# Seven block products for eight in a feed-forward layer: attention and two feed-forward blocks on one core

## Chip, core and metric

The kernel runs on one NeuronCore of a Trainium2 chip. TensorE (PE) multiplies matrices into PSUM, VectorE (DVE) and ScalarE (ACT) do the element-wise work, GpSimd (POOL) helps in the attention part, SyncE (SP) issues most DMAs. The metric is the device time of one execution in microseconds; lower is better.

## What is computed

Attention over 2 batches and 8 heads (query rows averaged in pairs, 576 queries against 1152 keys, head size 64) gives x of 1152 tokens by 512. Two feed-forward blocks follow:

```python
# first block
h = x @ w_in                      # 512 -> 2048
P = a[0] + a[1]*h + a[2]*h**2 + a[3]*h**3
Q = 1 + |b[0]|*|h| + |b[1]|*h**2
x = (P / (Q + 1e-6)) @ w_out      # 2048 -> 512
# second block
h = x @ w_in2                     # 512 -> 2048
g = max(h, 0) + log1p(exp(-|h|))  # softplus
out = g @ w_out2                  # 2048 -> 512
```

The four weight matrices arrive as 64-bit floats; each is turned on the chip into fp32.

## The kernel before

All products of the feed-forward blocks are made of two-part numbers. A value v is kept as `hi`, its rounding to the matmul type fp32r, and `lo`, the rest v - hi. A product a·b is three matmuls: hi·hi, lo·hi, hi·lo. Tokens are cut into three chunks c of 384 (`TOK`), the 2048 hidden columns into 16 slices f of 128 (`NF`), the 512 model columns into four slices d of 128 (`ND`).

The second block is the stage that the change touches. Its loop (line 1494) goes over 48 units (c, f). For one unit `up2` (L1343) makes h of 128 x 384 in one PSUM bank by 12 matmuls of 384 columns (four d times three). `act2` then has ScalarE take the softplus out of PSUM (L1351) and cast it to `gh` (L1352), and VectorE subtract to `gl` (L607, called through `sub`). Two units later `down2` (L1365) multiplies: for each of three token tiles t, three matmuls of 512 columns into the accumulator `acc[c, t]`. Units come as chunks 2 and 1 for f 0 to 7, chunk 0 for f 0 to 7, then f 8 to 15 chunk by chunk. `half2` puts the sums of chunks 1 and 2 after eight f into SBUF (L1374, L1376), and `end2` adds them in at the end (L1386) and sends the result out (L1391). Of the eight PSUM banks two hold h tiles (pool `ph2`) and six hold accumulators (`pa2`).

Weights come one tile (one f of w_in2 or w_out2) at a time while the loop runs. `w_load` (L643, L648) brings 512 KB into one of two staging tiles `wraw`; `w_abs` has ScalarE scale the upper halves into `pk` (L655); `w_conv` has VectorE shift and merge the bits (L663, L666, L669), after which the staging tile is free for the next load; `w_split` has ScalarE cast the hi part (L679) and VectorE subtract the lo part (L607). `w_step` moves each of these steps forward by one tile, and is called after units at the rate `r2` (90 in a hundred).

The tile framework orders each engine's instructions when the kernel is built, by its own estimates and priorities, and each engine then works through its list strictly in that order. So an instruction that waits holds up all that stand behind it on its engine.

The first block ends with `down1` (L1311) and `end1` (L1330, L1335, L607), which write the second block's input as `xh` and `xl`.

Of the kernel before, what the change touches and what calls it, by code (L numbers as in the profile page):

```python
# [7 lines left out]
F32 = mybir.dt.float32  # L8
# [24 lines left out]
    l2=1,  # L33
# [5 lines left out]
    rq=6,  # L39
# [447 lines left out]
def attn_moe_kernel(tc, q, k, v, w1_in, w1_out, moe_a, moe_b, w2_in, w2_out, out):  # L487
# [16 lines left out]
    LAG1, LAG2 = T["l1"], T["l2"]  # L504
# [122 lines left out]
    for m, lag in ((0, 2 * LAG1), (1, 2 * LAG2)):  # L627
        for lo, hi in ((0, NF // 2), (NF // 2, NF)):
            for f in range(lo, hi + lag, 2):
                if f < hi:  # L630
                    order += [(m, 0, f), (m, 0, f + 1)]
                if f >= lo + lag:
                    order += [(m, 1, f - lag), (m, 1, f - lag + 1)]
    NW = len(order) // 2
    NP1 = 4
# [36 lines left out]

    def w_split(i, pool, lo):
        g = st.pop(("pk", i)).bitcast(F32)
        w = pool.tile([128, 2, 512], F32R, tag="w", name="w")
# [569 lines left out]
    ph_ = pa_ = ap = wl_ = pt_ = pt2 = wpk = None  # L1245
# [91 lines left out]

    def up2(c, f):
        h = ph_.tile([128, 512], F32, tag="h2", name="h2")[:, 0:TOK]
# [7 lines left out]
    def act2(n, h):  # L1347
        if n % 2 == 0:
            st["g2"] = T_("p", 2), T_("gh", 2, F32R), T_("gl", 2, F32R)
        p, gh, gl = (t[:, n % 2] for t in st["g2"])  # L1350
        nc.scalar.activation(out=p, in_=h, func=AF.Softplus)  # L1351
        st["last", "gh"] = nc.scalar.copy(out=gh, in_=p).ins  # L1352
        sub(nc.vector, gl, p, gh)
        return gh, gl

    def down2(c, f, gh, gl, ts=(0, 1, 2)):
        first = f == 0 or (f == FH and c > 0)
        last = f == NF - 1 or (f == FH - 1 and c > 0)
        if first:
            for t in range(TOK // 128):  # L1360
                st["acc", c, t] = pa_.tile([128, DM], F32, tag="acc", name="acc")
        w = st["w", (1, 1, f)]
        for t in ts:
# [4 lines left out]
    def half2(c):  # L1368
        p = st["part2", c] = pt2[c - 1].tile([128, TOK // 128, DM], F32, name=f"part2{c}")
        for t in range(TOK // 128):  # L1370
            acc = st.pop(("acc", c, t))
            with tc.high_priority():
                if t == 1:
                    nc.vector.tensor_copy(out=p[:, t], in_=acc)  # L1374
                else:
                    nc.scalar.copy(out=p[:, t], in_=acc)  # L1376

    def end2(c, t):
        acc = st.pop(("acc", c, t))
        r0 = c * TOK + t * 128  # L1380
        both = T_("m", 2)
        for e in range(2):
            o = both[:, e, 0:DM // 2]
            es = slice(e * DM // 2, (e + 1) * DM // 2)
            if c:
                nc.vector.tensor_add(out=o, in0=acc[:, es], in1=st["part2", c][:, t, es])  # L1386
            elif e:
                nc.vector.tensor_copy(out=o, in_=acc[:, es])
            else:
                nc.scalar.copy(out=o, in_=acc[:, es])  # L1390
            (nc.sync, nc.scalar)[e if c == NCH - 1 else 0].dma_start(out=out[r0:r0 + 128, es], in_=o)  # L1391

    if True:
# [9 lines left out]
        wl_ = sb(name="wlast", bufs=NW - NP1 - NE - NRA - NRB)  # L1403
        pt_ = sb(name="part", bufs=1)

        freed = [st["wra"]] * max(0, NE + NRA - len(T["wt"]))
        freed += [st["wrb"]] * min(NRB, NE + NRA + NRB - len(T["wt"]))
        freed += [wl_] * (NW - NP1 - NE - NRA - NRB)
        n0 = len(T["wt"])
        cnt = {"load": n0, "abs": n0, "conv": n0, "split": n0}  # L1410

        def w_step():
            if cnt["split"] < cnt["conv"] and freed:
                w_split(cnt["split"], freed.pop(0), nc.vector)
                cnt["split"] += 1
            if cnt["conv"] < cnt["abs"]:
# [33 lines left out]
        for k in range(NG + LAG1):  # L1450
            if k == NG - 1:
                st["second"] = True
            if k < NG:
                for c, f in units[2 * k:2 * k + 2]:
# [3 lines left out]
                    if c == (NCH - 1 if f < FH else 0):  # L1458
                        freed.append(st["wp", (0, 0, f)])
# [11 lines left out]
            if k >= LAG1:  # L1471
                for e, (c, f) in enumerate(units[2 * (k - LAG1):2 * (k - LAG1) + 2]):
# [4 lines left out]
                    if c == (NCH - 1 if f < FH else 0):  # L1477
                        freed.append(st["wp", (0, 1, f)])
# [6 lines left out]
        pt2 = [sb(name=f"part2{c}", bufs=1) for c in range(2)]  # L1485
# [4 lines left out]
        units = [(c, f) for f in range(FH) for c in (2, 1)]  # L1490
        units += [(0, f) for f in range(FH)]
        units += [(c, f) for c in range(NCH) for f in range(FH, NF)]
        g2 = {}
        for n in range(NU + 2 * LAG2):
            if n < NU:
                c, f = units[n]
                if c == (NCH - 1 if f < FH else 0):
                    w_need((1, 0, f))
                g2[n] = act2(n, up2(c, f))
                if f < FH and c == 0:  # L1500
                    freed.append(st["wp", (1, 0, f)])
                if every(n, T["r2"]):
                    with tc.issue_after(st["last", "gh"]):
                        w_step()
            m = n - 2 * LAG2
            if m >= 0:
                c, f = units[m]
                if c == (NCH - 1 if f < FH else 0):
# [56 lines left out]
```

## Time and profile before

| what | value |
|---|---|
| median of 3 runs (lowest, highest) | 705.6 us (705.17, 705.92) |
| the profiled execution | 705.37 us |
| its span, first to last instruction | 703.5 us |
| PE busy, matmuls | 682.0 us (97% of the span), 4076 |
| DVE busy | 558.7 us (79%) |
| ACT busy | 494.3 us (70%) |
| mean granted TensorE clock | 0.993 of full speed |

The table is the profiler's account of one execution. Busy time is the time in which an engine had an instruction running. Matmuls overlap in the records, so a busy PE says little of how many matmuls it gets through; how far apart they start says more.

### The profile page before, as it was taken

Reading aid. Unit: us, or ns where it says so; the run is one execution under the profiler, and the core shown is the slowest. Engines: PE = TensorE matmul, PEld = TensorE weight load, DVE = VectorE, ACT = ScalarE, POOL = GpSimd, SP = SyncE. Lnnn points to the kernel's source line nnn. Section 1 sums busy time; section 2 is a strip of 40 time slices with the busy share of each in tenths; the row PEclk is TensorE's granted clock in tenths of the full one; section 3 lists DMA queues with packets and bytes.
Section 4 is the critical chain, followed back from the end, with each engine's and each line's share of the span. In section 5 each row is a group of like instructions: output and inputs, shape, how many; then the busy total and the mean of one; then the engine's idle time right before and its main releaser. Section 6 shows DMA issues by size and latency. Waiting matters only on the chain.

```text
span 703.5 us, 11809 instructions
## 1 busy us (share of the span) xinstructions
PE 682.0 (97%) x4076; PEld 630.0 (90%) x4076; DVE 558.7 (79%) x1082; ACT 494.3 (70%) x1135; POOL 196.8 (28%) x357
## 2 busy tenths in 40 slices
PE   7999999999999988989999999999999999999997
PEld 6898989898889867979999999999989999999996
DVE  5899999999898998699999999999777775631122
ACT  4989999999999987777777778766655454532221
POOL 4777767676857644400000000000000000000000
PEclk9999999999999998999999999999999999999999
DMA  4582837474747331122111122110054332301011
GB/s 131 147 208 56 184 72 183 90 180 106 172 98 182 97 118 64 61 64 86 31 61 60 62 93 87 61 60 1 11 171 149 120 120 90 121 1 45 1 46 45
DMA packets 60396, 65.68 MB, mean 93 GB/s; under 512 B 21553, under 2 KB 49457, under 8 KB 60337
## 3 DMA queue, kind: packets, MB, share of 16 engines
q1 hardware_dynamic: 59152, 63.95, 33.4%
q10 hardware_dynamic: 1184, 0.98, 0.4%
q8 instruction: 32, 0.52, 0.3%
q14 instruction: 28, 0.22, 0.1%
HBM read 47.71 MB, written 2.36 MB: 71 GB/s over the span
## 4 chain that ended last, share of the span: by engine, by line
PE 47%; DVE 6%; ACT 4%; DMA 3%; issue 1%; DVEq 0%; ACTq 0%; SPq 0%
PE acc L1365 13%; PE h L1343 12%; PE acc L1311 10%; PE h L1262 10%; DMA wraw<-in_moe_w_in_dram 2%; DMA wraw<-in_moe_w_out_dram 1%; PE pv L854 1%; PE t L725 1%; DVE m L1297 1%; ACT s L1292 1%; DVE p L1296 1%; ACT s L1291 1%; DVE m L1287 1%; DVE p L1285 1%; DVE pk L669 0%
## 5 line engine op out<-in xcount | busy, mean ns | idle before, releaser
L774 ACT ACTIVATE p<-s,mb 128x384 f32<-128x384 f32 x216 | 124.5, 590 | 4.1 <-DVE mb L765 3.6
L761 DVE TENSOR_REDUCE nm<-s 128x1 f32<-128x384 f32 x216 | 112.0, 549 | 9.7 <-PE s L754 8.7
L607 DVE TENSOR_TENSOR gl<-p,gh 128x384 fp32r<-128x384 f32 (+1 forms) x72 | 49.7, 690 | 80.6 <-ACT gh L1352 79.3
L725 PE MATMUL t<-ident,p 128*128 128x128 f32 x648 | 101.6, 277 | 4.2 <-ACT p L774 2.1
L1262 PE MATMUL h<-xh,w 128*128 128x384 f32 x384 | 98.1, 335 | 2.7 <-DVE p L1286 2.7
L1343 PE MATMUL h<-xh,w 128*128 128x384 f32 x384 | 98.7, 336 | 0.0
L1311 PE MATMUL acc<-gh,w 128*128 128x384 f32 x384 | 93.9, 337 | 1.3 <-ACT gh L1272 1.2
L1351 ACT ACTIVATE p<-h 128x384 f32<-128x384 f32 x48 | 23.5, 491 | 99.1 <-PE h L1343 99.1
L725 PEld LDWEIGHTS t<-ident,p 128*128 128x128 f32 x648 | 79.2, 142 | 13.5 <-ACT p L774 9.0
L1365 PE MATMUL acc<-w,gh 128*128 128x512 f32 x288 | 90.0, 393 | 0.3 <-DVE w L607 0.2
L854 PE MATMUL pv<-ph,v 128*128 128x256 f32 (+1 forms) x288 | 90.1, 326 | 0.0
L607 DVE TENSOR_TENSOR pl<-t,ph 128x384 fp32r<-128x384 f32 (+1 forms) x160 | 79.0, 511 | 7.7 <-ACT ph L717 4.8
L854 PE MATMUL pv<-pl,v 128*64 128x256 f32 (+1 forms) x288 | 76.6, 296 | 0.0
L607 POOL TENSOR_TENSOR pl<-c,ph 128x384 fp32r<-128x384 f32 (+1 forms) x80 | 73.5, 926 | 3.2
L717 ACT CAST ph<-t 128x384 fp32r<-128x384 f32 (+1 forms) x160 | 69.1, 466 | 7.5 <-PE t L725 6.0
L1343 PEld LDWEIGHTS h<-xh,w 128*128 128x128 f32 x384 | 70.4, 188 | 4.0 <-ACT p L1351 0.4
L1262 PEld LDWEIGHTS h<-xh,w 128*128 128x128 f32 x384 | 69.0, 188 | 3.8 <-issue 3.3
L1311 PEld LDWEIGHTS acc<-gh,w 128*128 128x128 f32 x384 | 68.5, 188 | 3.5 <-ACT gh L1272 3.3
L1343 PE MATMUL h<-xl,w 128*128 128x384 f32 x192 | 64.7, 337 | 0.0
L1262 PE MATMUL h<-xl,w 128*128 128x384 f32 x192 | 64.2, 334 | 0.0
L1365 PEld LDWEIGHTS acc<-w,gh 128*128 128x128 f32 x288 | 53.4, 188 | 10.2 <-DVE w L607 0.7
L1311 PE MATMUL acc<-gl,w 128*128 128x384 f32 x192 | 59.9, 336 | 0.0
(129 smaller groups left out, 1470.0 us busy)
## 6 DMA issues: line engine op xcount, KB each, us to landing
wraw<-in_moe_w_in_dram SPq DMA_DIRECT2D x32, 512.0 KB, 3.9
wraw<-in_moe_w_out_dram SPq DMA_DIRECT2D x32, 512.0 KB, 3.3
vr<-in_v_dram SPq DMA_DIRECT2D x8, 576.0 KB, 6.3
kr<-in_k_dram SPq DMA_DIRECT2D x15, 288.0 KB, 5.1
qr<-in_q_dram SPq DMA_DIRECT2D x15, 256.0 KB, 4.4
out_dram<-m SPq DMA_DIRECT2D x15, 128.0 KB, 1.7
qq1a<-qhi SPq DMA_DIRECT2D x8, 144.0 KB, 2.5
ks1a<-khi SPq DMA_DIRECT2D x4, 288.0 KB, 3.2
```

The lines of the kernel that those rows point to most:

```text
L607: return eng.tensor_tensor(out=o, in0=a, in1=b, op=ALU.subtract)
L717: nc.scalar.copy(out=out, in_=in_)
L725: nc.tensor.transpose(o[0:rows, i * 128:i * 128 + n], a, ident[0:n, 0:n])
L761: op("M" + str(n % 3), "DVE", fn=lambda: nc.vector.tensor_reduce(out=NM[i][:, n:n + 1], in_=tl[k], axis=AX.X, op=ALU.max, negate=True), R= ...
L774: nc.scalar.activation(out=o, in_=tl[k], func=AF.Exp, bias=MB[i][:, t:t + 1], accum_out=DEN[i][:, n:n + 1])
L854: nc.tensor.matmul(out=o, lhsT=p, rhs=r[:, m, 0:w], start=(c == a == 0), stop=(c == C - 1 and a == 1))
L1262: nc.tensor.matmul(out=h, lhsT=w[:, wi, wd], rhs=x[:, d, xcols(c)], start=(n == 0), stop=(n == 3 * ND - 1))
L1285: nc.vector.tensor_mul(out=p, in0=h, in1=p)
L1311: nc.tensor.matmul(out=st["acc", c, d], lhsT=w[:, wi, wd], rhs=g, start=(first and n == 0), stop=(last and n == 2))
L1343: nc.tensor.matmul(out=h, lhsT=w[:, wi, d * 128:(d + 1) * 128], rhs=x[:, d, xcols(c)], start=(n == 0), stop=(n == len(mm) - 1))
L1351: nc.scalar.activation(out=p, in_=h, func=AF.Softplus)
L1365: nc.tensor.matmul(out=st["acc", c, t], lhsT=g[:, t * 128:(t + 1) * 128], rhs=w[:, wi], start=(first and n == 0), stop=(last and n == 2))
```

## The change

For f of 4 to 15, and chunks 1 and 2 together, two slices f and f+1 are treated as the rows of a 2 x 2 block matrix A, whose columns are the halves d = 0, 1 and d = 2, 3. The input is a 2 x 2 block matrix B: rows are the same halves, columns are the chunks 1 and 2. One block product is six matmuls of 384 columns (two d times three). Four result blocks took eight such products, 48 matmuls; Strassen's scheme in Winograd's form takes seven, 42. It needs sums of blocks beforehand: four of B (`x_sums`, tiles T, once), four of A for each pair of f (`w_sums`, tiles S), each again cut into hi and lo; and seven additions on VectorE out of PSUM for each pair (`fast2`). Chunk 0 and f 0 to 3 stay with `up2`.

The block now runs in four groups of four f. In each group all three chunks are done, and the accumulators of every chunk are added into SBUF (`add2`) at the group's end. PSUM is four banks of h and four of accumulators. The parameters `l2` of before goes; `l2`, `d0`, `x0`, `hp` now say by how many units the second product trails the first and when the sums of B are made; `rq` lets one more weight step into the first block. The tiles of the last nine weights of the first block lie in another pool than before, and the second block's weights go into tiles that come free.

```diff
     l1=2,
-    l2=1,
+    l2=6,
+    d0=(0, 0, 0, 1, 1, 2, 2, 3, 4, 5, 6, 7),
+    x0=2,
+    hp=0,
...
-    rq=6,
+    rq=5,
...
+    GF = 4
+    for lo in range(0, NF, GF):
+        for kind in range(2):
+            order += [(1, kind, f) for f in range(lo, lo + GF)]
...
+    def w_sums(fa, fb):
+        ga, gb = (st.pop(("fp", f)) for f in (fa, fb))
+        t = st["S", fa] = ws_.tile([128, 2, 4, 256], F32R, tag="S", name="S")
+        a = st["St", fa] = tp_.tile([128, 4, 256], F32, tag="St", name="St")
+        lo, hi = slice(0, 256), slice(256, 512)
+        nc.vector.tensor_add(out=a[:, 0], in0=gb[:, lo], in1=gb[:, hi])
+        sub(nc.vector, a[:, 1], a[:, 0], ga[:, lo])
+        sub(nc.vector, a[:, 2], ga[:, lo], gb[:, lo])
+        sub(nc.vector, a[:, 3], ga[:, hi], a[:, 1])
+
+    def w_sums_split(fa):
+        t, a = st["S", fa], st.pop(("St", fa))
+        nc.scalar.copy(out=t[:, 0], in_=a)
+        sub(nc.vector, t[:, 1], a, t[:, 0])
...
+        def split(n, x):
+            t = st["T", n]
+            def fn():
+                with tc.issue_after(st["last", "gh"]):
+                    nc.scalar.copy(out=t[:, 0], in_=x)
+            steps.append(fn)
+            steps.append(lambda: sub(nc.vector, t[:, 1], x, t[:, 0]))
+
+        term(a, B[0][1][0], B[0][0][0], ALU.subtract)
+        term(a, a, B[0][1][1], ALU.add)
+        term(a, a, B[0][0][1], ALU.subtract)
+        term(b, B[1][1][0], a, ALU.subtract)
+        term(b, b, B[1][1][1], ALU.add)
+        split(0, a)
+        term(a, B[1][0][0], b, ALU.subtract)
+        term(a, a, B[1][0][1], ALU.add)
+        split(1, b)
+        term(b, B[1][1][0], B[0][1][0], ALU.subtract)
+        split(3, a)
+        term(b, b, B[1][1][1], ALU.add)
+        term(b, b, B[0][1][1], ALU.subtract)
+        split(2, b)
...
+    def products(o, a, b):
+        mm = [(wi, xi, d) for d in range(2) for wi, xi in ((0, 0), (1, 0), (0, 1))]
+        for n, (wi, xi, d) in enumerate(mm):
+            nc.tensor.matmul(out=o, lhsT=a[:, wi, d * 128:(d + 1) * 128], rhs=b[xi][:, d],
+                             start=(n == 0), stop=(n == len(mm) - 1))
...
+    def fast2(f):
...
+        o = prod("11", "11")
+        nc.scalar.copy(out=p1[:, 0], in_=o)
+        o = prod("S2", "T2")
+        V.tensor_add(out=v, in0=o, in1=p1[:, 0])
+        o = prod("S1", "T1")
+        V.tensor_add(out=p2[:, 1], in0=o, in1=v)
+        o = prod("S4", "22")
+        V.tensor_add(out=p2[:, 0], in0=o, in1=p2[:, 1])
+        o = prod("S3", "T3")
+        V.tensor_add(out=p2[:, 1], in0=o, in1=p2[:, 1])
+        V.tensor_add(out=v, in0=o, in1=v)
+        nc.scalar.activation(out=p2, in_=p2, func=AF.Softplus)
+        split2(p2, *g2)
+        o = prod("22", "T4")
+        V.tensor_add(out=p1[:, 1], in0=o, in1=v)
+        o = prod("12", "21")
+        V.tensor_add(out=p1[:, 0], in0=o, in1=p1[:, 0])
+        nc.scalar.activation(out=p1, in_=p1, func=AF.Softplus)
+        split2(p1, *g1)
...
+    def add2(c, f, t):
+        acc, p = st.pop(("acc", c, t)), st["part2", c][:, t]
+        with tc.high_priority():
+            if f >= GF:
+                nc.vector.tensor_add(out=p, in0=acc, in1=p)
+            elif t == 1:
+                nc.vector.tensor_copy(out=p, in_=acc)
+            else:
+                nc.scalar.copy(out=p, in_=acc)
...
-        ph_ = sb(name="ph2", bufs=2, space=PSUM)
-        pa_ = sb(name="pa2", bufs=2 * (TOK // 128), space=PSUM)
...
+        ph_ = sb(name="ph2", bufs=4, space=PSUM)
+        pa_ = sb(name="pa2", bufs=4, space=PSUM)
...
+        ups = [(c, f) for f in range(GF) for c in (2, 1)] + [(0, f) for f in range(GF)]
+        downs = [(c, f) for c in (2, 1, 0) for f in range(GF)]
+        for lo in range(GF, NF, GF):
+            ups += [(None, f) for f in range(lo, lo + GF, 2)] + [(0, f) for f in range(lo, lo + GF)]
+            downs += [(c, f) for c in (1, 2, 0) for f in range(lo, lo + GF)]
```

Three places show what each engine's list holds now. The first is TensorE in the middle of the second block. Before, units of 12 matmuls (tile h2) alternate with nine of the second product (acc):

```order
L1343 MATMUL h2_7210<-xh_74,w_7007 128x384 x2
L1343 MATMUL h2_7210<-xl_75,w_7007 128x384
L1365 MATMUL acc_6941<-w_7191,gh_7113 128x512 x2
L1365 MATMUL acc_6941<-w_7191,gl_7114 128x512
L1365 MATMUL acc_6942<-w_7191,gh_7113 128x512 x2
```

Now, in the first call of `fast2` (f = 4 and 5), the fifth product (S3 times T3, tile T2 by its index) is cut in two, and second products of chunk 0 stand between its matmuls:

```order
L1398 MATMUL h2_7310<-T2_6846,S_7065 128x384 x2
L1478 MATMUL acc_7380<-w_6895,gh0_7131 128x512
L1478 MATMUL acc_7380<-w_6895,gl0_7132 128x512
L1478 MATMUL acc_7384<-w_6895,gh0_7131 128x512 x2
L1398 MATMUL h2_7310<-T2_6846,S_7065 128x384
```

In all, h2 takes 540 matmuls where it took 576, and acc 432 as before. The second place is VectorE just ahead of that product. Before, its list there held only the lo part of g and the steps of a weight tile:

```order
L607 TENSOR_TENSOR gl_7114<-p_7112,gh_7113 128x384
L607 TENSOR_TENSOR w_7153<-pk_7086,w_7153 128x512
L663 TENSOR_SCALAR pk_7159<-pk_7159 128x512
L666 SCALAR_TENSOR_TENSOR pk_7159<-wraw_7126,pk_7159 128x512
L607 TENSOR_TENSOR w_7191<-pk_7124,w_7191 128x512
```

Now sums of weights (St), sums of the input (part20, the scratch of `x_sums`) and evacuations (part21) stand among them, and the lo part of T2 comes last:

```order
L672 SCALAR_TENSOR_TENSOR pk_7102<-wraw_7076,pk_7102 128x512
L1368 TENSOR_TENSOR part20_6841<-part20_6841,xl_75 128x768
L675 SCALAR_TENSOR_TENSOR pk_7102<-wraw_7076,pk_7102 128x512
L1368 TENSOR_TENSOR part20_6841<-part20_6841,xl_75 128x768
L610 TENSOR_TENSOR gl0_7132<-p_7130,gh0_7131 128x384
L610 TENSOR_TENSOR gl0_7213<-p_7211,gh0_7212 128x384
L610 TENSOR_TENSOR w_7217<-pk_7102,w_7217 128x512
L1487 COPY part21_6842<-acc_7190 128x512
L610 TENSOR_TENSOR T2_6846<-part20_6841,T2_6846 128x768
```

The lo part of T2 is the 72nd VectorE instruction of the second block in the list. The third place is VectorE at the end of the third call of `fast2` (f = 8 and 9), where the evacuations of chunk 2 (part22) stand between the two lo parts of that call and the sums of weights for f = 10; there was no such place before:

```order
L1464 TENSOR_TENSOR p_7694<-h2_7745,v_7700 128x384
L610 TENSOR_TENSOR gl2_7699<-p_7697,gh2_7698 128x768
L1485 TENSOR_TENSOR part22_6843<-acc_7647,part22_6843 128x512
L610 TENSOR_TENSOR gl1_7696<-p_7694,gh1_7695 128x768
L1485 TENSOR_TENSOR part22_6843<-acc_7651,part22_6843 128x512
```

The last row is the 159th of the block; it frees the bank that the third accumulator of chunk 0 (f = 4 to 7) takes.

## Rows read from the trace of the kernel before

**Rows 1.** Page, part 2: busy tenths in 40 slices of 17.6 us; PEclk: granted clock.

```profile
PE   7999999999999988989999999999999999999997
...
DVE  5899999999898998699999999999777775631122
...
PEclk9999999999999998999999999999999999999999
```

**Rows 2.** Chain that ended last, second block: start us, us, engine, what.

```profile
528.22 2.10 PE h L1343 x12
530.33 2.08 PE acc L1365 x9
...
691.51 8.21 PE acc L1365 x36
```

**Rows 3.** Timeline, TensorE from the last matmul of block 1, and the end: start us, us.

```profile
499.31 0.34 PE L1311 MATMUL acc<-gl,w 128*128 128x384 f32 x1
499.49 0.33 PE L1343 MATMUL h<-xh,w 128*128 128x384 f32 x1
...
699.33 0.39 PE L1365 MATMUL acc<-w,gl 128*128 128x512 f32 x1
```

**Rows 4.** Groups by form, second block: count | busy us, mean ns | idle before.

```profile
L607 DVE TENSOR_TENSOR gl<-p,gh 128x384 fp32r<-128x384 f32 x48 | 26.8, 558 | 79.3 <-ACT gh L1352 79.3
...
L1351 ACT ACTIVATE p<-h 128x384 f32<-128x384 f32 x48 | 23.5, 491 | 99.1 <-PE h L1343 99.1
L607 DVE TENSOR_TENSOR w<-pk,w 128x512 fp32r<-128x512 f32 x30 | 20.7, 691 | 0.9 <-ACT w L679 0.9
...
L663 DVE TENSOR_SCALAR pk<-pk 128x512 int32<-128x512 int32 x28 | 11.8, 422 | 3.3 <-ACT pk L655 3.3
L1386 DVE TENSOR_TENSOR m<-acc,part 128x256 f32<-128x256 f32 x12 | 4.5, 420 | 9.6 <-PE acc L1365 8.3 <-DMA out_dram<-m 1.3
```

**Rows 5.** Groups by form, first block: the 768-wide lo and hi parts of g.

```profile
L607 DVE TENSOR_TENSOR gl<-p,gh 128x768 fp32r<-128x768 f32 x24 | 22.9, 954 | 1.3 <-ACT gh L1272 1.2
...
L1272 ACT CAST gh<-p 128x768 fp32r<-128x768 f32 x24 | 20.1, 836 | 5.9 <-DVE p L1298 5.9
```

**Rows 6.** Timeline of VectorE: start us, us, what.

```profile
446.00 0.95 DVE L1297 SCALAR_TENSOR_TENSOR m<-m,s 128x768 f32<-128x768 f32 x1
446.87 0.95 DVE L1285 TENSOR_TENSOR p<-h,p 128x768 f32<-128x768 f32 x1
...
502.98 0.55 DVE L607 TENSOR_TENSOR gl<-p,gh 128x384 fp32r<-128x384 f32 x1
...
504.38 0.70 DVE L607 TENSOR_TENSOR w<-pk,w 128x512 fp32r<-128x512 f32 x1
504.99 0.42 DVE L663 TENSOR_SCALAR pk<-pk 128x512 int32<-128x512 int32 x1
505.44 0.69 DVE L666 SCALAR_TENSOR_TENSOR pk<-wraw,pk 128x512 int32<-128x512 int32 x1
506.05 0.55 DVE L607 TENSOR_TENSOR gl<-p,gh 128x384 fp32r<-128x384 f32 x1
506.52 0.69 DVE L607 TENSOR_TENSOR w<-pk,w 128x512 fp32r<-128x512 f32 x1
```

**Rows 7.** Waits, 500 to 530 us: who for whom, us in total, times, longest.

```profile
DVE pk L663 <- ACT pk L655: 3.3, 5, 1.3
...
ACT pk L655 <- DMA wraw<-in_moe_w_out_dram: 1.7, 2, 1.4
...
DVE w L607 <- ACT w L679: 0.9, 2, 0.7
```

**Rows 8.** Windows: busy us by engine, granted clock, DMA share, GB/s.

```profile
440.00:460.00 20.00, 20.00 (x116) 19.75 (x116) 20.00 (x28) 14.62 (x20) 0.00 (x0) 1.00 0.17 53
520.00:530.00 10.00, 9.69 (x49) 8.27 (x48) 8.13 (x16) 4.85 (x9) 0.00 (x0) 1.00 0.40 118
630.00:640.00 10.00, 10.00 (x52) 9.04 (x51) 1.78 (x4) 3.43 (x9) 0.00 (x0) 1.00 0.16 53
```

More of the change, by code (lines that the diff above doesn't have):

```diff
@@ L1345, in up2, with pair2 @@
         return h
[L1347 to L1351, printed above, removed]
-        st["last", "gh"] = nc.scalar.copy(out=gh, in_=p).ins
[L1353 to L1360, printed above, removed]
+    def pair2(c, f):
+        p = p2_.tile([128, 2, TOK], F32, tag="p", name="p")
+        g = tuple(g2_.tile([128, 2, TOK], F32R, tag=f"{n}{c}", name=f"{n}{c}") for n in ("gh", "gl"))
+        for e in range(2):
+            st["g", c, f + e] = tuple(x[:, e] for x in g)
+        return p, g
@@ L1361, in down2 @@
+    def down2(c, f, ts=(0, 1, 2)):
+        first, last = f % GF == 0, f % GF == GF - 1
+        w = st["w", (1, 1, f)]
+        gh, gl = st["g", c, f]
+        for t in ts:
+            if first:
                 st["acc", c, t] = pa_.tile([128, DM], F32, tag="acc", name="acc")
-        w = st["w", (1, 1, f)]
-        for t in ts:
             for n, (g, wi) in enumerate(((gh, 0), (gh, 1), (gl, 0))):
@@ L1494, in attn_moe_kernel @@
[L1494 to L1503, printed above, removed]
-                        w_step()
[L1505 to L1508, printed above, removed]
-                    w_need((1, 1, f))
-                if c < NCH - 1 or f < NF - LAST:
-                    down2(c, f, *g2[m])
-                    if f < FH and c == 0:
-                        freed.append(st["wp", (1, 1, f)])
-                    if f == FH - 1 and c:
-                        half2(c)
-                    if f == NF - 1:
-                        for t in range(TOK // 128):
-                            end2(c, t)
@@ new lines, in attn_moe_kernel, with down_next @@
+        steps = x_sums()
+        def down_next():
+            c, f = downs.pop(0)
+            w_need((1, 1, f))
+            if c == 0 and f == NF - GF:
+                while steps:
+                    steps.pop(0)()
+                for t in range(TOK // 128):
+                    for e in range(GF):
+                        down2(0, f + e, ts=(t,))
+                    end2(0, t)
+                downs.clear()
+                return
+            down2(c, f)
+            if c == 0:
+                w_free((1, 1, f))
+            if f % GF == GF - 1:
+                for t in range(TOK // 128):
+                    (end2 if f == NF - 1 else lambda c, t: add2(c, f, t))(c, t)
@@ new lines, in attn_moe_kernel @@
+        u = d = 0
+        for c, f in ups:
+            st["u"] = u
+            w_need((1, 0, f + (c is None)))
+            if c is None:
+                while f in st["sf"] or ("S", f) not in st:
+                    w_step()
+                fast2(f)
+            else:
+                act2(c, f)
+                if c == 0:
+                    w_free((1, 0, f))
+            for _ in range(4 if c is None else 1):
+                u += 1
+                if every(u, T["r2"]):
+                    with tc.issue_after(st["last", "gh"]), tc.issue_after(st["last", "gl"]):
+                        w_step()
+                for _ in range(2 if u >= T["x0"] else 0):
+                    if steps:
+                        with tc.issue_after(st["last", "gl"]):
+                            steps.pop(0)()
+            while d < (T["d0"][u - 1] if u <= len(T["d0"]) else u - T["l2"]):
+                d += 1
+                down_next()
```

161 lines of the change are left out of this document (108 added, 53 removed).

## Prediction

> **What bounds the kernel now.** Read the page's slices first. From the middle of the span on, PE stands at 9 of ten in nearly every slice and the granted clock is full, while VectorE falls from 9 to 7 and then to 1 [rows 1]. In the second block the chain of waits is PE alone: 12 matmuls of the first product in 2.10 us, nine of the second in 2.08 us, in turn, to the end [rows 2]. So matmuls start 175 ns (384 columns) and 231 ns (512 columns) apart, and these two numbers are what a matmul costs. The groups tell the same from the other side: ScalarE idles 99.1 us in front of the softplus waiting for h, and VectorE 79.3 us waiting for gh [rows 4]. Both are paced by PE there. But not all along: in 520 to 530 us VectorE is busy 8.13 of 10 us, in 630 to 640 us 1.78 [rows 8], because the weights are converted in the first half of the block.
>
> **How far PE is from its own limit.** Block 1's last matmul starts at 499.31 us, and the second block has PE to itself from 499.49; its last matmul starts at 699.33, so its slot ends at 699.56 [rows 3]. In these 200.07 us stand 566 matmuls of 384 columns (576 less ten issued earlier) and 432 of 512: 566 x 0.175 + 432 x 0.2315 = 199.06 us. PE loses 1.0 us. What follows the last slot, addition and output, takes 3.94 us to the end of the 703.5 us span. The profiled execution is 705.37 us, 1.87 us over its span and 0.23 us under the median of 705.6.
>
> **Removed.** Six pairs of f each lose six matmuls of 384 columns: 36 x 0.175 = 6.3 us, all of it on PE, which sets the end. The Trainium skill (TensorE: Matmul & The Clock Gate, Back-to-back issue gap) gives N/2.4 + 2.5 ns per matmul, 162.5 ns for 384 columns, and the saving would be 5.9 us; the trace has 175 ns [rows 2], and its number is used. With 530 and 432 matmuls PE needs 192.76 us from 499.49 on. Without any stall its last slot would end at 692.25, the span at 696.19 and the execution at 698.06, or 698.3 against the median. That is 7.3 us gained, the lost 1.0 us included. Every stall of PE comes on top.
>
> **Added on VectorE.** Costs are starts, not durations: VectorE starts its next instruction 0.47 us after a 384-wide one (recorded as 0.55), 0.61 after a 512-wide (0.69), 0.45 after a shift and 0.87 after a 768-wide one (0.95) [rows 6]. From these, 256 wide is 0.35 us and 1024 wide 1.14, by the slope of 1.04 ns per element. The second block's list now holds 66 instructions 384 wide (42 of them the additions out of PSUM), 105 of 512, 28 shifts, 26 of 768, 42 of 256 and six of 1024: 31.0 + 64.1 + 12.6 + 22.6 + 14.7 + 6.8 = 152 us. Before, the same stretch held 48 of 384, 88 of 512 (three for a weight tile), 28 shifts and some 15 of 256, about 94 us. VectorE has 200 us, so in sum there is room. In time there is not, for the new work lies in the first half, where the weights are. ScalarE was busy 4.85 of 10 us there [rows 8] and takes over nothing that fills it.
>
> **First tight place: the sums.** The fifth product of the first `fast2` needs the lo part of T2, the 72nd VectorE instruction. Up to it stand 11 of 384, nine shifts, 29 of 512, 14 of 768, eight of 256, one of 1024: 5.2 + 4.0 + 17.7 + 12.2 + 2.8 + 1.1 = 43.0 us, from 502.98, the first lo part of g [rows 6]; the last one's record ends 0.1 us after its successor could start. It is ready at 546.1 if VectorE never waits. PE in front of that matmul has 160 matmuls of 384 columns and 77 of 512: 45.8 us, so it arrives at 545.3. PE waits 0.8 us at the least. What VectorE waits for on the way is bounded by two rows: in the first block it is busy 20.00 of 20 us [rows 8], that is no wait; between 500 and 530 us before, it waited 3.3 us for ScalarE's `w_abs`, which itself waited 1.7 us for loads, and 0.9 us for the hi parts of weights [rows 7], 4.2 us in all. The load chain is the same now: two staging tiles, each load freed by VectorE's last merge. But sums of the input now stand between the merges and fill such waits. I take 2 us, nearer to the first block's row. PE's loss here: 2.8 us.
>
> **Second tight place: the turn of the accumulators.** With four banks instead of six, an accumulator can start only when the fourth before it has been added into SBUF. Most of these turns have a unit of 12 matmuls (2.1 us) between; the worst I find is the third accumulator of chunk 0, f 4 to 7. It needs the 159th VectorE instruction, which stands behind the lo parts of the third `fast2`. The 87 instructions from the 73rd on take 48.4 us by the same starts. In each `fast2` the two 768-wide lo parts wait for a softplus and a cast of that width on ScalarE. The cast takes 0.84 us [rows 5]; for the softplus I take 0.8, since 0.49 at 384 wide [rows 4] grows as the cast does. Other work covers about half of these waits: 1.2 us left in each of three calls. So 546.1 + 2 + 48.4 + 3.6 = 600.1. PE gets there after 308 matmuls of 384 columns and 186 of 512, at 596.45, plus the 2.8 lost: 599.2. Another 0.9 us.
>
> **Costed at nothing.** The seven additions of a `fast2` are 3.3 us beside seven products of 7.35 us; with four h banks each product needs the evacuation of the one four products back. If VectorE is behind, that cover goes, and the lateness is the one already counted. The extra weight step in the first block is one 512-wide subtraction, 0.6 us, where VectorE is full; PE has units in store there. The evacuations at a group's end (18 additions, 11 us in sum) are inside the 152 us. The tail has the same shape as before.
>
> **Sum.** 698.3 + 2.8 + 0.9 = 702.0 us against the median of 705.6. With VectorE's lower bound, no wait anywhere, it is 699.1; with the upper one (4.2 us before T2 and some 2 more than mine after it) 706.2, worked out below.
>
> **The rivals.**
> *Nothing is late.* VectorE waits half a microsecond before T2, and the turns are covered: 1.3 us lost, 699.6 us. For it speaks the first block's full VectorE; against it that ScalarE's part of a weight must come between.
> *The old waits stay.* VectorE waits 4.2 us on the way to T2, as it did between 500 and 530 us, and 2 us more for weights up to the turn: T2 at 550.3, 5.0 late; the turn at 604.3 against 601.5, another 2.8. That is 706.1 us, no change that a measurement (about 0.2%, 1.4 us) could tell. For it speaks that the two staging tiles are the same; against it the new work that fills such waits.
> *VectorE costs its durations.* If each instruction takes the whole of its recorded time, as where each depends on the one before, the 72 take 47.9 us instead of 43.0 (0.558, 0.42, 0.69, 0.955, 0.42 us each [rows 4, 5], and 1.22 for the 1024-wide one by their slope); with 2 us of waits T2 is ready at 552.9, 7.6 us late, and up to the turn 54.5 us instead of 48.4 and the waits of 3.6 make it 611.0 against 604.1: 14.5 us lost, 712.8 us, slower. It decides from the point where VectorE takes 6% more than its starts: then the turn is 8.7 us late and the kernel above 707.0. The rows speak against it where neighbours are independent, since starts then lie closer than durations, and for it where the next reads the one before: the merge starts 0.03 us after the shift's recorded end [rows 6]. The list mostly puts independent ones side by side. The Trainium skill (VectorE: DVE Perf Modes, The DRAIN you can't avoid) says the next operation cannot issue until the pipe is empty, exceptions apart; by that rule this rival is the forecast, and the trace disagrees.
> That the products are not fewer is no rival: the list has 540 where 576 stood.
>
> **Chances.** Forecast (2 to 5.9 us lost) 0.56, nothing late 0.17, old waits 0.16, durations 0.11. Faster by over 0.2% is the first two, 0.73; within it 0.16; slower 0.11. The range of 699.2 to 706.0 leaves out the durations and the far ends of the others.
>
> **What would show it.** Right: 540 matmuls on h, 175 ns apart in groups of six; gaps of PE in front of the fifth product of the first `fast2` (some 3 us by then, waiting for VectorE) and around the second group's end (about 1 us); VectorE near 9 of ten from 500 to 620 us; hardly a gap of PE after 650 us, where the last weight tile is through. Wrong: gaps of PE at every `fast2` (the additions chain is then the bound, not the sums), VectorE idle while PE waits (then ScalarE or the loads), a granted clock under full after a gap, or a late end of block 1.

## The result, and the profile after

| | kernel before | changed kernel |
|---|---|---|
| median of the runs, us | 705.52 (6 runs, 704.83 to 705.92) | 697.89 (6 runs, 695.86 to 698.62) |
| ratio, 95% interval | | 0.9887 (0.9871 to 0.9902) |
| profiled execution, us; its span | 705.37; 703.5 | 696.2; 694.3 |
| mean granted clock of that span | 0.993 | 1.0 |

The change is worth 7.6 us, about twice the 3.6 us that were forecast, and the time lies under the forecast range. The page's slices of the changed kernel (17.4 us each) answer to [rows 1]:

```profile
PE   7999999999999988989999999999999999999997
...
DVE  5899999999899999799999999999799999888722
...
PEclk9999999999999999999999999999999999999999
```

In the second block VectorE's row of 7, 7, 7, 7, 5, 6, 3, 1, 1 (from the 30th slice on) has become five of 9, three of 8 and a 7, as forecast; PE is as full as before. So the new work of VectorE is there, and PE hardly feels it. TensorE's timeline of the changed kernel (start us, us, line, what) gives the second block's beginning and end, against [rows 3]:

```profile
497.63 0.33 PE L1334 MATMUL acc<-gl,w 128*128 128x384 f32 x1
497.80 0.33 PE L1409 MATMUL h<-xh,w 128*128 128x384 f32 x1
...
690.18 0.39 PE L1478 MATMUL acc<-w,gl 128*128 128x512 f32 x1
```

From 497.80 to the end of the last slot (690.18 + 0.23) are 192.6 us, where 200.1 stood before: 7.5 us. The block begins 1.7 us earlier too, and that is another matter (the third experiment below). The chain that ended last (start us, us, what) shows what it consists of, against [rows 2]:

```profile
582.81 7.30 PE h L1398 x42
590.11 8.20 PE acc L1478 x36
598.32 7.30 PE h L1398 x42
...
676.25 14.34 PE acc L1478 x63
```

42 matmuls of 384 columns in 7.30 us are 173.8 ns each, 36 of 512 in 8.20 us 227.8 ns, 63 in 14.34 us 227.6 ns. These are the two prices of a matmul in long, undisturbed runs. [Rows 2] had 175 and 231 ns, from runs of 12 and 9. With the two prices every start of a matmul in the second block can be held against the start before it. What exceeds them by over 60 ns is called "lost" in this table, the rest "spread":

| second block, us | length | matmuls at 0.1738 and 0.2276 | spread | lost |
|---|---|---|---|---|
| before | 200.1 | 566 and 432: 196.7 | 2.2 | 1.2 |
| changed kernel | 192.6 | 530 and 432: 190.4 | 1.25 | 0.9 |

The 7.5 us are 6.3 of matmuls, 0.9 of closer spacing and 0.3 of stalls. Of the 0.9 us lost, 0.7 lie at one place. ScalarE's timeline points to its cause (the last bracket of a row is the idle time in front of it and what ended it), and TensorE's the effect:

```profile
563.67 0.66 ACT L661 ACTIVATE pk<-wraw 128x512 f32<-128x512 f32 x1 [3.88 <-DMA wraw<-in_moe_w_in_dram]
564.24 0.83 ACT L1461 ACTIVATE p<-p 128x768 f32<-128x768 f32 x1
565.10 0.84 ACT L1421 CAST gh<-p 128x768 fp32r<-128x768 f32 x1
```

```profile
567.60 0.96 PE L1478 MATMUL acc<-w,gh 128*128 128x512 f32 x3 [0.15 <-ACT gh L1421]
568.60 0.50 PE L1478 MATMUL acc<-w,gl 128*128 128x512 f32 x1
```

ScalarE stands 3.9 us in front of a weight's first conversion step until its load lands, and the softplus of the second seven-product pair is queued behind it. This is read from the trace; no run shows the block without this queue.

### The profile page after: what moved, and what is told of

Read it like the earlier page. It is cut to its first block, busy times and chain, and to the rows that moved or that the text cites. A ratio compares the mean times of both kernels' runs of the same rounds, so it can differ in the third digit from the quotient of the medians.

```text
span 694.3 us, 11815 instructions
## 1 busy us (share of the span) xinstructions
PE 671.7 (97%) x4040; PEld 619.7 (89%) x4040; DVE 610.7 (88%) x1177; ACT 502.9 (72%) x1126; POOL 197.4 (28%) x357
## 4 chain that ended last, share of the span: by engine, by line
PE 38%; DVE 12%; ACT 4%; DMA 4%; issue 2%; POOL 1%; DVEq 0%; ACTq 0%; SPq 0%
PE acc L1478 14%; PE h L1409 7%; PE acc L1334 6%; PE h L1285 5%; PE h L1398 5%; DMA wraw<-in_moe_w_in_dram 3%; DVE m L1310 1%; DVE m L1320 1%; DVE p L1308 1%; DVE p L1319 1%; DVE p L1321 1%; DVE p L1309 1%; DVE pk L675 1%; DVE w L610 1%; DMA wraw<-in_moe_w_out_dram 1%
## 5 line engine op out<-in xcount | busy, mean ns | idle before, releaser
L1285 PE MATMUL h<-xh,w 128*128 128x384 f32 x384 | 98.0, 335 | 2.8 <-DVE p L1309 2.8
L1285 PEld LDWEIGHTS h<-xh,w 128*128 128x128 f32 x384 | 69.0, 188 | 3.9 <-issue 3.4
L1285 PE MATMUL h<-xl,w 128*128 128x384 f32 x192 | 64.2, 334 | 0.0
L610 DVE TENSOR_TENSOR gl<-p,gh 128x768 fp32r<-128x768 f32 (+1 forms) x60 | 47.5, 793 | 16.5 <-ACT gh L1421 14.8
L877 PEld LDWEIGHTS pv<-ph,v 128*128 128x128 f32 x288 | 54.2, 188 | 2.6 <-ACT c L847 1.2
L1478 PE MATMUL acc<-w,gl 128*128 128x512 f32 x144 | 56.3, 393 | 0.0
L1409 PE MATMUL h<-xh,w 128*128 128x384 f32 x192 | 49.3, 336 | 0.0
L702 ACT CAST w<-pk 128x512 fp32r<-128x512 f32 x52 | 32.1, 622 | 21.2 <-DVE pk L675 21.1
```

What stands on the lines that cost most here:

```text
L610: return eng.tensor_tensor(out=o, in0=a, in1=b, op=ALU.subtract)
L877: nc.tensor.matmul(out=o, lhsT=p, rhs=r[:, m, 0:w], start=(c == a == 0), stop=(c == C - 1 and a == 1))
L1285: nc.tensor.matmul(out=h, lhsT=w[:, wi, wd], rhs=x[:, d, xcols(c)], start=(n == 0), stop=(n == 3 * ND - 1))
L1409: nc.tensor.matmul(out=h, lhsT=w[:, wi, d * 128:(d + 1) * 128], rhs=x[:, d, xcols(c)], start=(n == 0), stop=(n == len(mm) - 1))
L1478: nc.tensor.matmul(out=st["acc", c, t], lhsT=g[:, t * 128:(t + 1) * 128], rhs=w[:, wi], start=(first and n == 0), stop=(last and n == 2))
```

## The experiments

All times below are medians; "block 2" is the length from the second block's first matmul to the last slot's end in the profiled execution, as above, and "block 1 starts" is the start of the first block's first matmul there. Runs of one group share a chip and the runs of the kernel before.

| run | us | ratio to before, 95% | block 1 starts | block 2 | lost |
|---|---|---|---|---|---|
| before | 705.52 | | 290.6 | 200.1 | 1.2 |
| changed kernel | 697.89 | 0.9887 (0.9871 to 0.9902) | 288.6 | 192.6 | 0.9 |
| eight | 702.83 | 0.9965 (0.9953 to 0.9978) | 292.4 | 197.9 | 0.1 |
| dose14 | 704.44 | 0.9994 (0.9978 to 1.001) | 290.1 | 199.35 | 7.7 |
| fill_before | 704.26 | 0.9987 (0.9974 to 1.0) | 288.2 | 200.5 | 1.7 |
| fill_after | 696.86 | 0.9877 (0.9856 to 0.9897) | 288.5 | 192.7 | 1.0 |
| after_again | 698.02 | 0.9894 (0.9878 to 0.991) | 290.1 | 192.5 | 0.8 |
| dose7 | 703.72 | 0.9974 (0.996 to 0.9987) | 289.9 | 198.1 | 6.3 |
| abs_pool | 711.97 | 1.0092 (1.0076 to 1.0107) | 290.7 | 206.5 | 14.5 |
| best | 710.76 | 1.0071 (1.0052 to 1.009) | 289.7 | 208.2 | 16.2 |
| dose2 | 698.72 | 0.9912 (0.989 to 0.9933) | 290.9 | 192.65 | 1.0 |
| fill_att | 696.81 | 0.9879 (0.9864 to 0.9894) | 288.9 | 192.7 | 1.0 |
| fill_more | 697.98 | 0.9897 (0.9882 to 0.9911) | 289.2 | 192.8 | 1.1 |

The kernel before had medians of 704.98 us beside the first group (eight, dose14, fill_before, fill_after), 705.50 beside the second (after_again, dose7, abs_pool, best) and 705.45 beside the third.

**Eight products in the new grouping (eight).** What is the seven products' part, and what the regrouping's?

```diff
-                while f in st["sf"] or ("S", f) not in st:
-                    w_step()
-                fast2(f)
+                for x in range(2):
+                    for y in (2, 1):
+                        act2(y, f + x)
...
-        steps = x_sums()
+        steps = []
```

> The changed kernel's four groups of four f, homes and order of weights, but chunks 1 and 2 of f 4 to 15 by eight products, without the sums of inputs and weights and without the additions out of PSUM. Theory A (the saving is the 36 matmuls, 0.175 us each, and nothing is given back on VectorE): 6.3 us over the changed kernel, 704.2 us, and PE loses at most half a microsecond in the second block, as in the changed kernel; of the gain over the kernel before, the new grouping then has about 1 us (its lost 1.0 us). Theory B (the new grouping and the banks bring more than the products): within 4 us of the changed kernel, under 702. Theory C (the seven products give something back on VectorE that the eight do not): more than 0.5 us less than 6.3 us over the changed kernel.

Block 2 takes 197.9 us, 5.3 more than in the changed kernel, so theory C holds by size: 6.3 us of matmuls, of which the seven products give 1.0 back (0.8 of it the stalls, 0.1 against 0.9 lost). Its place is not VectorE, though: 0.7 of the stalls is the one behind ScalarE's queue, above. Theory B is out. And the regrouping alone (with its banks and its order of the weights, which no run takes apart), 200.1 to 197.9 us, brings 2.2 us: 1.1 of stalls and 1.1 of closer spacing. Longer runs of one kind are what it makes; its chain reads

```profile
654.07 8.34 PE h L1409 x48
662.42 8.20 PE acc L1478 x36
```

that is 173.8 and 227.8 ns again. Start by start, the spread of this run and of the kernel before lies at the head of each run of one kind, by the same amounts: about 22 ns over the first six matmuls of 384 columns and 33 ns over the first nine of 512. Further in, a matmul stands at its price. The kernel before has 43 runs of either kind, this one 26 (the changed kernel 34), which makes some 0.95 of the 1.1 us. Why the head of a run costs more is not shown. This run also tells what VectorE does without the sums. Its windows (length, busy us of PE, PEld, DVE, ACT and POOL, granted clock, DMA share, GB/s), and below those of the changed kernel:

```profile
510.00:520.00 10.00, 10.00 (x55) 9.43 (x54) 8.34 (x16) 6.36 (x12) 0.00 (x0) 1.00 0.48 144
520.00:530.00 10.00, 10.00 (x53) 9.08 (x52) 8.59 (x16) 6.87 (x14) 0.00 (x0) 1.00 0.55 170
530.00:540.00 10.00, 10.00 (x51) 8.96 (x50) 7.64 (x15) 5.91 (x11) 0.00 (x0) 1.00 0.34 111
```

```profile
510.00:520.00 10.00, 10.00 (x53) 9.21 (x53) 10.00 (x16) 7.03 (x14) 0.00 (x0) 1.00 0.44 134
520.00:530.00 10.00, 10.00 (x53) 9.13 (x52) 10.00 (x20) 6.97 (x14) 0.00 (x0) 1.00 0.36 107
530.00:540.00 10.00, 10.00 (x54) 9.25 (x53) 10.00 (x18) 4.85 (x9) 0.00 (x0) 1.00 0.31 105
```

Without sums VectorE idles 5.4 of these 30 us, with them not at all. In eight its waits for ScalarE's part of a weight are still there, 500 to 540 us:

```profile
DVE pk L669 <- ACT pk L661: 2.8, 4, 1.1
```

In the changed kernel the sums of the input and the weights fill these holes.

**More work for VectorE (dose14, dose7, dose2).** How near is VectorE to being the bound?

```diff
+DOSE = {u: 2 for u in range(2, 9)}
...
+                for _ in range(DOSE.get(u, 0)):
+                    with tc.issue_after(st["last", "gl"]):
+                        nc.vector.tensor_tensor(out=dz, in0=xh[:, 0, 0:TOK].bitcast(F32), in1=xl[:, 0, 0:TOK].bitcast(F32), op=ALU.add)
```

dose7 has one addition at each of these units, dose2 one at units 2 and 5 alone.

> The changed kernel with 14 more additions, 384 wide, on VectorE between units 2 and 8 of the second block (0.47 us each from start to start, 6.6 us, 15% on the 43 us of the way to T2), their result unused. In the changed kernel's trace the last part of T2 is written 0.4 us ahead of the matmul that wants it, and an accumulator is added into SBUF 0.4 us ahead of the one that takes its bank. Theory A (PE stands in a fixed order, so what VectorE is later PE loses): 6.2 us more, 704.1 us. Theory B (the order of the instructions is laid out anew around VectorE's time, and PE has other matmuls to go ahead with): the matmul that wants T2 moves back by 4.9 us in the order of PE, T2 is 1.1 us late there, and the kernel loses 1 to 3 us, 699 to 701 us. Theory C (VectorE has room anyway, 152 of 192 us): no loss.

> The changed kernel with 7 more additions, 384 wide, on VectorE between units 2 and 8 of the second block (3.3 us). 14 of them (6.6 us) cost 6.7 us in the second block: 5 us of waits of PE and 1.8 us of a clock that fell to 0.50 behind the waits. Theory A (VectorE is the second bound there, with some 0.4 us to spare and no more): 2.5 to 3 us of waits in the second block, 195.1 to 195.6 us, and more by up to 2 us if the clock falls again. Theory B (the order of the instructions, which the scheduler lays out anew, moves the matmul that wants T2 back by 3.5 us, and T2 is 0.8 us ahead of it): under 1 us, 192.6 to 193.6 us.

> The changed kernel with 2 more additions, 384 wide, on VectorE, at units 2 and 5 of the second block (0.9 us). Seven of them lengthened the second block by 5.5 us, fourteen by 6.7. Theory A (VectorE's slack there is 0.4 us, and each lateness over it goes to PE): 0.5 to 1 us more in the second block, 193.1 to 193.6 us. Theory B (seven reached a point from which waits add up, an idle PE and then half the clock; under it the order takes up small latenesses): 192.5 to 192.8 us, no change.

0.9 us more on VectorE cost block 2 nothing (theory B of dose2), 3.3 us cost 5.5 (4.0 of waits, about 1.5 of a lower clock), 6.6 us cost 6.7. For 14 additions the size is theory A's, but the place is not T2: its lo part is in time, written by 551.1 us for a matmul that starts at 551.38. PE's waits of dose14, 497 to 600 us (who for whom, us in total, times, longest):

```profile
PE h L1399 <- DVE v L1454: 1.9, 1, 1.9
PE acc L1479 <- ACT gh L1422: 1.8, 1, 1.8
PE acc L1479 <- DVE gl L611: 1.0, 1, 1.0
```

A lo part of g ahead of T2 is late by 1.0 us. The additions of the first `fast2` come late, so the sixth product (22 times T4) finds no free h bank (1.9 us), and the softplus that waits for the additions is late for the second layer (1.8 us). Then another cost follows, which no theory had. Its windows in the same columns as above:

```profile
560.00:562.00 2.00, 0.39 (x2) 0.34 (x3) 1.28 (x2) 1.97 (x3) 0.00 (x0) 1.00 0.00 0
562.00:564.00 2.00, 2.00 (x7) 1.63 (x6) 2.00 (x4) 1.98 (x4) 0.00 (x0) 0.50 0.00 0
564.00:566.00 2.00, 2.00 (x8) 1.73 (x7) 2.00 (x5) 0.00 (x0) 0.00 (x0) 0.65 0.00 0
```

PE is busy 0.39 of 2 us, and behind that the granted clock stands at 0.50 (1.2 GHz). The matmuls from 561.6 to 566 us take 1.7 us more than at the two prices. In dose7 PE waits 0.9 us for an evacuation at 530 us and 3.1 us for that softplus, with a fall of the clock at the same point:

```profile
558.00:562.00 4.00, 0.96 (x4) 0.79 (x5) 2.27 (x4) 3.91 (x6) 0.00 (x0) 0.97 0.00 0
562.00:566.00 4.00, 4.00 (x14) 3.48 (x13) 4.00 (x7) 1.78 (x4) 0.00 (x0) 0.60 0.00 0
```

Theory B of dose7 is right that T2 would not be late and wrong about the sum: what is late is what follows T2. So the kernel begins to lose somewhere between 0.9 and 3.3 us of added work. At 3.3 us PE loses more than VectorE's lateness, at 6.6 us about as much; each dose has one profile, and its order is laid out anew. The run of dose2 was 0.8 us slower than the changed kernel, but its block 2 is the changed kernel's, to 0.1 us; in its profile the clock fell at 271 us, ahead of the first block.

**The clock ahead of the first block (fill_before, fill_after, fill_att, fill_more, after_again).** Block 1 starts 2.0 us earlier in the changed kernel's profile, though every engine's instructions up to there are the same in both kernels. The windows of the kernel before and, below, of the changed kernel:

```profile
268.00:272.00 4.00, 2.32 (x12) 1.33 (x11) 3.80 (x10) 3.54 (x12) 0.63 (x4) 0.77 0.41 136
272.00:276.00 4.00, 4.00 (x18) 3.74 (x19) 2.47 (x6) 1.62 (x6) 0.34 (x1) 0.50 0.35 128
```

```profile
268.00:272.00 4.00, 2.17 (x12) 1.36 (x11) 3.83 (x10) 3.53 (x12) 0.92 (x4) 1.00 0.39 133
272.00:276.00 4.00, 3.77 (x28) 3.64 (x29) 3.31 (x11) 3.15 (x10) 1.13 (x3) 1.00 0.42 131
```

PE is busy 2.2 to 2.3 of 4 us in both; in the one the clock then falls to 0.50, and 18 matmuls stand in 4 us where 28 do in the other. Matmuls of zeros in those gaps test it:

```diff
+FILL = {("S", 7, 15): 10, ("T", 7, 12): 5, ("T", 7, 14): 10, ("S", 7, 18): 14}
...
+    def keep(k, key):
+        for _ in range(FILL.get(key, 0)):
+            nc.tensor.matmul(out=st["full", k][0:64, 384:512], lhsT=zero[:, 0:64], rhs=zero[:, 0:128], start=True, stop=True)
```

fill_att has three more places (5, 14 and 9 matmuls, 247 to 257 us), fill_more 30 matmuls besides at the first block's fourth unit; after_again is the changed kernel itself.

> The changed kernel with 39 matmuls of zeros (128 columns, into unused columns of score and transpose banks) behind four instructions of the last attention pair, at about 266 to 272 us, where TensorE stands idle for 0.4 to 1 us four times and where the granted clock fell to 0.50 in the profile of the kernel before and did not in that of the changed kernel. The instructions of all engines up to there are the same in both. Theory A (the 1.7 to 2 us that the two profiles differ by ahead of the first block are this fall of the clock, which comes in some executions): no fall between 260 and 280 us, and all times near 696, none at 698. Theory B (they are not the clock's): times at 696 and at 698 as without them. If the fill is too short the fall stays, and both are open.

> The same 39 matmuls of zeros in the kernel before. Theory A (the fall of the clock at 270 us costs it 2 us in nearly every execution): 703.5 us, 2 us under the kernel before, and the changed kernel with the same fill is 7.3 us under this one, which is what PE needs less in the second block. Theory B (the clock is no cause): no change, 705.5 us.

> The changed kernel once more, to have its times on the same chip as those of the next three, and a second profile. Theory A (what the change is worth stands in the second block alone; what differs ahead of it is the clock's, by chance): the second block takes 192.6 us again, from its first matmul to its last slot's end, while the start of the first block lies anywhere between 288 and 292 us, late where the granted clock falls at 270 us. Theory B (the first 1.7 us belong to the change): the first block starts at 288.6 us again.

> The changed kernel with 67 matmuls of zeros (128 columns, into unused columns) behind the instructions of the attention's last two pairs where TensorE then stands idle for half a microsecond or more: 247, 249 and 257 us beside the four places at 266 to 272 us. In nine profiles with these gaps open the clock fell behind one of them seven times. The order on all other engines is as in the changed kernel. Theory A (each fall of the clock stands behind a wait of PE, and a fall costs what PE then does at half the clock): no fall before 290 us; times 695.3 to 697, most under the changed kernel's 698. Theory B (the falls do not depend on PE's waits): they come as often as before, and the median is 698.

> The same with 30 matmuls of zeros more at the first block's start, where PE waits 2.0 us for VectorE at 297 to 299 us, into unused columns of an h bank. The scheduler then lays out the first block a little differently. Theory A: no fall of the clock anywhere, 695.3 to 696.3 us. Rival: the matmuls of zeros, or the other order in the first block, hold up what they stand in front of, and the first block takes longer than 209.3 us, up to 2 us.

(The text of fill_att counts nine profiles. By the traces, ten had at least the gaps at 247 to 257 us open, and in seven of them the clock fell behind one of the gaps.) The windows of fill_after:

```profile
268.00:272.00 4.00, 3.81 (x40) 2.84 (x38) 3.80 (x11) 3.62 (x11) 0.69 (x4) 1.00 0.44 137
272.00:276.00 4.00, 3.93 (x31) 3.73 (x30) 3.30 (x11) 3.14 (x10) 1.20 (x3) 1.00 0.41 131
```

Counting all profiles of this study: without the zeros the clock fell between 268 and 276 us in seven of eight, with them in none of five. The changed kernel's first profile is the one without a fall, and after_again has it: its block 1 starts at 290.1 us and its block 2, 192.5 us long, at 499.7, no earlier than in the kernel before: theory A of after_again. So the 1.7 us ahead of block 2 are not the change's. With the zeros in both kernels the change is worth 7.4 us (704.26 to 696.86), as fill_before's theory A said (7.3). What the fall costs the median is less than fill_before's theory A had: 705.0 to 704.3 us instead of 703.5, and the interval of the ratio (0.9974 to 1.0) reaches up to no gain. The times with the zeros still spread over 2.7 us (703.2 to 705.9); in the profiles the fall is also not equally long each time, and block 1 starts between 289.9 us (dose7, a short one) and 290.9 (dose2, a long one). For the changed kernel 697.9 and 698.0 us stand against 696.9 and 696.8 with the zeros; the intervals of the ratios overlap, so 1 us is likely and not shown. fill_att comes out nearly as its theory A had it (695.8 to 697.2 us, no fall ahead of 290 us in its profile); fill_after only in its profile, since it still has times at 697.5. In fill_att the clock falls at 300 us, behind the 2 us wait at the first block's start:

```profile
300.00:320.00 20.00, 19.42 (x103) 19.08 (x102) 19.37 (x27) 15.12 (x22) 0.00 (x0) 0.91 0.25 80
```

That one costs nothing: its block 1 takes 209.0 us, that of the changed kernel without any fall 209.2. fill_more, which fills that wait as well, is the rival's case: the first block is laid out anew and takes 210.0 us, with a fall of the clock at 307 us.

**A conversion step on GpSimd (abs_pool, best).** The one stall of 0.7 us is ScalarE's, held up by a load. Would it go if the step that waits for the load stood on an idle engine? best is abs_pool with fill_after's zeros.

```diff
-            nc.scalar.activation(out=o, in_=hi, func=AF.Copy, scale=REBIAS)
+            nc.gpsimd.tensor_scalar(out=o, in0=hi, scalar1=REBIAS, scalar2=None, op0=ALU.mult)
```

> The changed kernel with the first step of the weights' conversion in the second block (27 scalings, 512 wide, 0.67 us each on ScalarE) on GpSimd, which has nothing else to do there. In the changed kernel ScalarE stands 3.9 us in front of one of them, until a weight lands, at 560 to 564 us, and the softplus of the second seven-product pair stands behind it; PE loses 0.7 us at 567 us, the largest of its stalls. Theory A (that stall is ScalarE's, held up by a load): it goes, the second block takes 191.8 to 192.0 us, 0.6 to 0.8 us less. Theory B (GpSimd's work holds up VectorE, which is full until 550 us, or comes later than ScalarE's): VectorE's parts get longer or the weights later, and the second block takes 193 us or more.

> The changed kernel with the 39 matmuls of zeros in the last attention pair and the first step of the weights' conversion on GpSimd. Theory A (both costs are there and are apart): the first block starts at 288.5 us, the second takes 191.9 us, and the time is 0.7 us under that of the kernel with the zeros alone, near 695.5 us where the clock is full. Theory B: no better than with the zeros alone.

Block 2 gets 14 us longer, theory B and far more than it said. GpSimd's step in abs_pool (ns: min/median/max) and what VectorE waits for, second block:

```profile
L661 POOL TENSOR_SCALAR pk<-wraw x27: 1511/1552/6239, 470.2 to 650.0; 128x512 f32<-128x512 f32 x27
```

```profile
DVE pk L669 <- POOL pk L661: 11.1, 8, 2.3
```

A step costs 1.55 us where ScalarE took 0.67, and up to 6.2; VectorE then waits for weights, and PE for VectorE and ScalarE. The Trainium skill (GPSIMD Engine Reference, When to use GPSIMD) puts one-input elementwise work on GpSimd at roughly line rate. For this step, which reads every second word, the trace disagrees; what makes it slow is not shown. So the experiment does not answer its question, the 0.7 us remain, and whether an earlier load would take them away was not tried.

The two runs show something else by the way. In both PE waits 2.5 us for VectorE, until 527.7 and 527.1 us. Behind the wait the clock stays up in abs_pool and falls in best, where it costs 1.7 us (abs_pool first, in the columns of above):

```profile
528.00:532.00 4.00, 4.00 (x20) 3.48 (x20) 3.86 (x9) 3.17 (x7) 1.71 (x1) 1.00 0.47 140
```

```profile
528.00:532.00 4.00, 4.00 (x14) 3.61 (x13) 3.86 (x9) 2.98 (x7) 2.04 (x2) 0.57 0.45 133
```

No version beats the changed kernel by more than its interval; fill_after and fill_att have the lowest medians of all.

## Why the prediction was wrong

**What bounds: right.** PE is the bound, its starts are the unit of account, and what is taken off it is taken off the time.

**Removed: right; that the others would stand closer was left out.** 36 matmuls fewer are 6.3 us. The price of 175 and 231 ns, though, was taken for all matmuls from runs of 12 and 9 [rows 2], with the longer run of 36 in 8.21 us in the same group. The regrouping makes longer runs, and the no-stall need is 191.7 us (190.4 and 1.25 of spread) instead of 192.76: 1.1 us that the forecast hadn't. The Trainium skill (TensorE: Matmul & The Clock Gate, Back-to-back issue gap) gives N/2.4 + 2.5 ns for the gap of a single matmul, by which one is estimated at 162.5 and 215.8 ns. The longest runs here stand at 173.8 and 227.8, so the trace's numbers were the right choice, only of too short runs.

**First tight place, 2.8 us: measured 0.** The mechanism was the right one: the last part of T2 is the 72nd instruction of VectorE's list. The two timelines of the changed kernel:

```profile
501.30 0.55 DVE L610 TENSOR_TENSOR gl<-p,gh 128x384 fp32r<-128x384 f32 x1
...
508.31 0.42 DVE L669 TENSOR_SCALAR pk<-pk 128x512 int32<-128x512 int32 x1
508.65 0.68 DVE L610 TENSOR_TENSOR w<-pk,w 128x512 fp32r<-128x512 f32 x1
...
542.33 0.95 DVE L610 TENSOR_TENSOR T<-part,T 128x768 fp32r<-128x768 f32 x1
543.19 0.42 DVE L669 TENSOR_SCALAR pk<-pk 128x512 int32<-128x512 int32 x1
```

```profile
542.44 0.51 PE L1398 MATMUL h<-T,S 128*128 128x384 f32 x2
...
543.71 0.69 PE L1398 MATMUL h<-T,S 128*128 128x384 f32 x3
```

VectorE takes 41.9 us for the 72 (501.30 to 543.19), and T2's lo part is written by 543.3; the matmul that wants it starts at 543.71, 45.9 us into the block, where the forecast had 45.8. So PE is 0.4 us later than VectorE, not 2.8 us earlier. Two sizes failed. The 2 us of waits were 0.1: the sums fill them, as the windows of eight and of the changed kernel show, and that was the very argument which the forecast named and then valued at half. The row to follow was the first block's 20.00 of 20 us [rows 8]. And a shift costs 0.34 us (508.31 to 508.65), not 0.45: in [rows 6] the merge behind it reads what it writes, here another instruction stands between. Nine of them are the other 1.0 us.

**Second tight place, 0.9 us: measured 0.** From the 73rd to the 159th instruction VectorE takes 51.8 us (543.19 to 594.99), of which it stands idle for 3.5; the forecast had 48.4 + 3.6. The timelines:

```profile
594.39 1.28 DVE L1485 TENSOR_TENSOR part<-acc,part 128x512 f32<-128x512 f32 x2
```

```profile
594.75 0.62 PE L1478 MATMUL acc<-w,gh 128*128 128x512 f32 x2
595.21 0.39 PE L1478 MATMUL acc<-w,gl 128*128 128x512 f32 x1
595.43 0.62 PE L1478 MATMUL acc<-w,gh 128*128 128x512 f32 x2
```

The 159th, the first of the two additions, ends near 595.1, and the third accumulator starts at 595.43. VectorE's part of the term was right and fell with the first: VectorE came to it 3 us earlier. The room is small, though. The 159th ends 0.35 us ahead of its matmul, and PE had lost 0.7 us at 567 us by then. Without that stall PE would have stood some 0.4 us here (an estimate from these two numbers), unless VectorE, which waited 0.7 us for the same weight at 564 us, had come earlier too.

**Costed at nothing.** Additions, evacuations and the tail (3.9 us before and after) cost nothing, as said. Not seen was ScalarE: its queue holds a softplus behind a weight's load, 0.7 us. The cover that was named for the additions (VectorE not behind) is real: dose14 takes it away and pays 1.9 us in front of the sixth product.

**The sum.** Forecast for the last slot's end was 499.49 + 192.76 + 3.7 = 695.95 us; it is 690.41. The 5.5 us between are, each rounded, 2.8 (3.7 us of stalls forecast, 0.9 found), 1.1 (spacing) and 1.7 (the clock ahead of the block, chance). In the medians the clock's part is mostly on both sides: 702.0 forecast against 697.9, of which 3.9 are the first two. That the sum without any stall, 698.3, lies so near the 697.9 is luck: the spacing that it lacks and the stalls that it leaves out are of about one size.

**The rivals.** "Nothing late" was the mechanism; its 699.6 us lacked the spacing. "Old waits stay" is out. "VectorE costs its durations" is out for this kernel. What a later VectorE costs is shown by the doses: 3.3 us more, 8% of the list to T2, made 703.7 us of 698. The rival's 707.0 at 6% is not borne out, since dose14, with 15%, is at 704.4: it started from a T2 that was 2.8 us late already. What made dose7's loss larger than the lateness itself is in part the clock, in part the queues behind the late additions. By the rule of the Trainium skill (VectorE: DVE Perf Modes, The DRAIN you can't avoid) the next instruction does not start until the pipe is empty; the same place says that one which is not held starts earlier. The trace shows the second of the two: 72 instructions take 41.9 us, where their recorded durations add up to 47.6.

## What to carry to other kernels

A wait that was measured where an engine had nothing else to do is not a price for that engine once it has a full list: take it only with the work that will stand in it. Take the price of an instruction from a row in which its neighbour depends on it as the new one will. And when two kernels' profiles differ ahead of the change, compare the granted clock there before giving the time to the change.

## What was not expected of the hardware

A stretch in which PE stands idle for parts of a few microseconds can cost twice: the wait, and then matmuls at half the clock. It does not always: of two waits of 2.5 us at the same place, in abs_pool and best, one had a fall behind it. In the attention's last pair (2.3 of 4 us busy) it put off the first block by some 1.7 us: it starts at 289.9 to 290.9 us in the profiles where the clock fell there and nowhere else in the last two pairs, at 288.2 to 289.2 where it fell nowhere in them. In the second block it had a part, about 1.5 us, in what made 5.5 us of VectorE's 3.3. A fall at 300 us, behind PE's wait for VectorE, cost nothing that the first block's length shows. Matmuls of zeros into unused columns kept the clock up between 268 and 276 us in all five profiles that had them there; elsewhere, where none stood, it still fell in four of the five ahead of the kernel's end.
